# A linear-attention kernel with two MLPs: the opening in another order, y moved between SBUF tiles, the later parts two steps on

## The chip, the cores and the metric

The kernel runs on one core of one Trainium2 chip. The metric is the time of one execution in device microseconds (us); the time before is the median of three runs. The engines are TensorE (PE, with its weight loads PEld), VectorE (DVE), ScalarE (ACT), GpSimd (POOL) and SyncE (SP), which here only issues DMA transfers.

## The reference

```python
def attn(q, k, v, alpha):          # B=4, H=8, S=768, D=48
    for t in range(S):
        state = alpha[:, :, t, :, None] * state + einsum('bhd,bhe->bhde', k[:, :, t], v[:, :, t])
        y[:, :, t] = einsum('bhd,bhde->bhe', q[:, :, t], state)
x = y.transpose(0, 2, 1, 3).reshape(3072, 384)
h = x @ w_in;   x = (h * sigmoid(1.702 * h)) @ w_out        # d_ff = 2048
h = x @ w_in2;  x = (h - tanh(h)) @ w_out2
```

## The kernel before, in words

The 768 tokens of each of the four batches are cut into six **chunks** of 128 tokens, 24 chunks in all. A chunk's attention is done with matmuls. DVE runs two scans over alpha (`a_scan`, L241), and scales k and q with the results (`a_scale`, L247 and L248, "the scale" below). PE makes the scores of the eight heads in two halves (`a_scores`, L277), ACT copies them out of PSUM (L282, L290), POOL masks them (L287). PE then makes the chunk's y and its share of the state (`a_out`, L306, L313, L322, "the sums" below), DVE updates the state (`a_state`, L333 to L336), ACT copies y out (`a_evac`, L341), and y goes by DMA into the DRAM tensor `xt` and from there, transposed, into the tile `xlo` (`a_back`, L359). ACT rounds it into `xhi` (L363), DVE leaves the remainder in `xlo` (`a_x`, L364). `a_guard` (L252, on ACT) squares the scanned alphas for a check at the end.

The two MLPs run behind and beside this in **steps**: one step is one block of 512 tokens (four chunks) with one of the sixteen tiles of 128 hidden columns; there are 6 x 16 steps for each MLP. A step `s` is `gemm1` (nine matmuls, L373: x and the weights are each split into a high and a low part of a shorter format, and three products are made), the activation on ACT (`sig_1`, L387), the split of its result (`g_split`, ACT L390 and DVE L391), and, three steps later, `gemm2` (nine matmuls, L380). `gemm1` of step s writes PSUM bank 3 or 4 in turn, so step s+2 needs the bank that the activation of step s has read.

The weights come as 64-bit numbers, a tile of 768 KB for each of the sixteen, into three `raw` buffers in turn (`w_load`, L154). DVE makes them into 32-bit numbers (`w_bits`, L161 and L162; `w_join`, L174, after which the `raw` buffer is free), ACT rounds the high part (L191), DVE subtracts the low part (L192). These four DVE instructions and the one of ACT are a **conversion**; in the first sixteen steps `conv` makes one in each step.

The code ahead of the steps is the **opening**: chunks 0 to 3, which fill the first block, and the first conversions. `idle(n)` puts n matmuls into it whose result nobody reads. In the first sixteen steps the parts of chunks 4 to 7 are mixed in (`attend`): a scan and the first half of the scores, a scan and the second half, the sums and the scale of the next chunk. `a_done` copies y out and loads the chunk after the next one. The order of these instructions on each engine is the program's own up to step 15 (`in_order`); after that a scheduler sets it.

All transfers go through SP's queue in program order. Each signals one of eight semaphores (DMAHW0 to DMAHW7); a transfer that gets a semaphore whose last transfer may still be under way waits for that one.

Of the kernel before, what the change touches and what calls it, by code (L numbers as in the profile page):

```python
# [7 lines left out]
F32 = mybir.dt.float32  # L8
# [60 lines left out]
def linear_attention_mlps(ctx, tc, xq, xv, fa, fv, cst, w1, w2, out):  # L69
# [106 lines left out]
    def w_any(l, m):  # L176
# [9 lines left out]
        A.copy(whi[m], f)  # L186
        G.tensor_tensor(out=wlo[m], in0=f, in1=whi[m].bitcast(F32), op=ALU.subtract)

    def w_split(l, m):
        f = cfs[l][m % len(cfs[l])]  # L190
        A.copy(whi[m], f)  # L191
        V.tensor_tensor(out=wlo[m], in0=f, in1=whi[m].bitcast(F32), op=ALU.subtract)  # L192

# [73 lines left out]
        V.tensor_scalar(out=flag, in0=bank[0][:1, :1], scalar1=DP + 255.5, scalar2=None, op0=ALU.is_lt)  # L267


    def a_scores(g, x, b):  # L270
        u = (2 * g + x) % 2
        q, k = qq(g), qkk(g)
        o = [bank[b + hh][:, : 2 * CE].rearrange("p (a t) -> p a t", a=2) for hh in range(2)]
        for i in range(2):
            for hh in range(2):
                r = slice(64 * hh, 64 * hh + D)
                P.matmul(out=o[hh][:, i], lhsT=k[r, 2 * x + i], rhs=q[r, 2 * x + i], start=True, stop=True)  # L277
        s4 = sm[u].rearrange("p (b a t) -> p b a t", b=2, a=2)
        kt = kts[u].rearrange("p (b a t) -> p b a t", b=2, a=2)
        for hh in range(2):  # L280
            if g < FULL:
                A.copy(s4[:, hh], o[hh][:, :, :C])  # L282
            else:
                V.tensor_tensor(out=s4[:, hh], in0=o[hh][:, :, :C], in1=mask.unsqueeze(1).to_broadcast([128, 2, C]), op=ALU.mult)
        if g < FULL:
            s3 = sm[u].rearrange("p (a t) -> p a t", a=4)
            G.affine_select(out=s3, in_=s3, pattern=[[0, 4], [1, C]], channel_multiplier=1, base=1 - C,  # L287
                            compare_op=ALU.is_ge, fill=0.0)
        for hh in range(2):
            A.copy(kt[:, hh], o[hh][:, :, C:])  # L290


    def a_out(g, b):
        c = g % NCH
# [40 lines left out]
            else:  # L335
                V.tensor_tensor(out=state, in0=dl, in1=al, op=ALU.mult)  # L336

    def a_evac(g, b):
        ys = ysb[g % 2 if g < FULL else 0]
        for hh in range(2):  # L340
            A.copy(ys[:DP, 2 * C * hh : 2 * C * hh + 2 * C], bank[b + hh][:DP, : 2 * C])  # L341
        y4 = ys.rearrange("p (b a t) -> p b a t", b=2, a=2)
        tk = slice(g * C, g * C + C)
        for n in range(2):
            for hh in range(2):
# [10 lines left out]
    def a_back(g):  # L356
        _, xl, o = a_at(g)
        tk = slice(g * C, g * C + C)
        SP.dma_start(out=xl[:, :, o].bitcast(F32), in_=xt.rearrange("h d t -> (h d) t")[:, tk].rearrange("(k p) t -> p k t", p=128))  # L359

    def a_x(g):
        xh, xl, o = a_at(g)
        A.copy(xh[:, :, o], xl[:, :, o].bitcast(F32))  # L363
        V.tensor_tensor(out=xl[:, :, o], in0=xl[:, :, o].bitcast(F32), in1=xh[:, :, o].bitcast(F32), op=ALU.subtract)  # L364


    def gemm1(i, m, h, n):
        xh, xl = xhi[i % 2], xlo[i % 2]
# [78 lines left out]
    def fetch():  # L447
        while due:
            w_load(*due.pop(0))

    def conv(layer, split=True):
        if split and cv[2] < cv[1]:
            w_split(layer, cv[2] % MT)
            cv[2] += 1
        if cv[1] < cv[0]:
            m = cv[1] % MT
            w_join(layer, m)
            cv[1] += 1
            if m + 3 < MT:
                due.append((layer, m + 3))  # L460
            if layer == 2:
                fetch()
        if cv[0] < min(layer * MT, cv[2] + len(cfs[layer])):
            w_bits(layer, cv[0] % MT)
            cv[0] += 1
# [11 lines left out]
    def a_done(g, b=5):  # L477
        a_evac(g, b)
        if g + 2 < NG:
            a_load(g + 2)  # L480
        if g < FULL:
            a_back(g)

    def attend(g, r, b=5):
        if r == 0:
# [28 lines left out]
    a_load(1, (0, 1))  # L514
    a_load(0, (4,))
    a_load(1, (2, 3, 4))
    a_load(2)
    w_load(1, 0)
    for b in (0, 1, 7):
        V.memset(bank[b], 0.0)  # L520
    V.memset(state, 0.0)
# [2 lines left out]
    for r in range(3):  # L524
        prep(0, r)
    idle(20)
    for g in range(4):
        for r in range(2):
            a_scores(g, r, (5, 3)[r])
        idle(6)  # L530
        if g == 2:
            w_bits(1, 0)
            w_join(1, 0)
            cv[:2] = 1, 1
        if g < 3:
            for r in range(3):
                prep(g + 1, r)
        if g == 3:
            conv(1)
            a_x(0)  # L540
            a_x(1)
            conv(1)
            prep(4, 0)
            prep(4, 1)
        a_guard(g)
        a_out(g, 0)
        idle((8, 4, 10, 36)[g])
# [32 lines left out]
    for s in range(NS + LAG):  # L580
# [19 lines left out]
        if s < NS:  # L600
            if l == 1 and j + 1 < len(L1):
                t1, n1 = L1[j + 1]
                if j:
                    parts, span = n1 // C * 4, 11
                    todo = range(min(parts, -(-m * parts // span)), min(parts, -(-(m + 1) * parts // span)))
                else:
                    todo = ((4 * (m // 3) + m % 3,) if m % 3 < 2 else (4 * (m // 3) + 2, 4 * (m // 3) + 3)) if m < 12 else ()
                for r in todo:
                    attend(t1 // C + r // 4, r % 4)
            if l == 1 and j == 0:  # L610
                sig_1(s, h, n)
                if m % 3 == 2 and m < 12:
                    a_done(m // 3 + 4)
                    a_state(m // 3 + 4)
                if m % 3 == 0 and 0 < m < 13:
                    prep(m // 3 + 4, 3)
                if m % 3 == 1 and m > 3:
                    a_x(m // 3 + 3)
# [138 lines left out]
```

## Time and profile before

| what | us |
|---|---|
| median of 3 runs | 958.71 (957.57 to 959.43) |
| the profiled execution's own time | 958.45 |
| its span in the profile | 956.4 |
| PE busy | 935.7 (98%) |
| DVE busy | 600.8 (63%) |
| ACT busy | 463.5 (48%) |

The shares are means over the whole span. The stretch that the change touches is the first 135 us of the 956, and there the engines stand otherwise to each other than in the mean: tables by stretch and rows in order of time show it. "Idle before" in a row is the pause of that engine ahead of the instruction, with what ended it. PEclk is the share of the full TensorE clock that was granted: 1.00 is 2.4 GHz, 0.50 is 1.2 GHz.

### The profile page before, as it was taken

The numbers are of one execution on the slowest core, as the hardware profiler recorded it, in microseconds if no ns is written. First come the engines' busy times: TensorE is split into PE (matmuls) and PEld (weight loads), VectorE is DVE, ScalarE is ACT, GpSimd is POOL, SyncE is SP. The second block draws the span as 40 slices with busy tenths as digits, with TensorE's granted clock in tenths as the row PEclk, the third lists the DMA queues.
The fourth block names the chain that finished last, engine by engine and source line by source line (L and its number), as shares of the span: only waits on it lengthen the run. The fifth ranks groups of instructions, "written<-read, shape, count | busy, mean of one in ns | idle before, by whom it ended". The sixth has DMA issues, their size and how long they took to land.

```text
span 956.4 us, 13247 instructions
## 1 busy us (share of the span) xinstructions
PE 935.7 (98%) x4972; PEld 726.5 (76%) x4972; DVE 600.8 (63%) x900; ACT 463.5 (48%) x970; POOL 86.6 (9%) x70
## 2 busy tenths in 40 slices
PE   8879999999999999999999999999999999999997
PEld 4457777777777777777788888888888888888885
DVE  6799954442454344733159986766777777766663
ACT  4455534434434444434344555545656656544542
POOL 2111211110110110010100200100101001000000
PEclk9979999999999999999999999999999999999999
DMA  9877423341635545741225400200322420000001
GB/s 231 243 242 233 135 72 106 85 130 41 211 114 186 159 129 177 279 115 50 80 103 168 159 37 1 96 5 0 131 90 78 165 99 1 34 1 1 34 1 38
DMA packets 58042, 101.84 MB, mean 106 GB/s; under 512 B 4992, under 2 KB 37376, under 8 KB 57968
## 3 DMA queue, kind: packets, MB, share of 16 engines
q1 hardware_dynamic: 57968, 100.90, 33.7%
q8 instruction: 41, 0.67, 0.3%
q14 instruction: 33, 0.27, 0.1%
HBM read 86.73 MB, written 14.16 MB: 105 GB/s over the span
## 4 chain that ended last, share of the span: by engine, by line
PE 93%; DVE 2%; DMA 2%; ACT 1%; issue 1%; POOL 0%; SPq 0%; DVEq 0%; ACTq 0%
PE bank L380 43%; PE bank L373 42%; PE bank L277 4%; PE bank L313 2%; PE bank L306 1%; PE bank L322 1%; DMA arena<-xq 1%; DMA cs<-cst 1%; POOL arena L287 0%; DMA xlo<-xt 0%; DVE arena L241 0%; DVE cf L174 0%; DVE cf L162 0%; DVE wlo L192 0%; DVE xlo L364 0%
## 5 line engine op out<-in xcount | busy, mean ns | idle before, releaser
L391 DVE TENSOR_TENSOR glo<-gt,ghi 128x512 fp32r<-128x512 f32 x192 | 139.4, 726 | 170.0 <-ACT ghi L390 166.8
L373 PE MATMUL bank<-xhi,whi 128*128 128x512 f32 x576 | 230.1, 400 | 1.9 <-ACT xhi L363 1.9
L373 PE MATMUL bank<-xlo,whi 128*128 128x512 f32 x576 | 229.1, 398 | 2.4 <-DVE xlo L364 2.4
L380 PE MATMUL bank<-ghi,whi 128*128 128x512 f32 x576 | 230.4, 400 | 0.0
L380 PE MATMUL bank<-ghi,wlo 128*128 128x512 f32 x576 | 229.2, 398 | 0.0
L373 PE MATMUL bank<-xhi,wlo 128*128 128x512 f32 x576 | 228.6, 397 | 0.0
L380 PE MATMUL bank<-glo,whi 128*128 128x512 f32 x576 | 228.2, 397 | 0.0
L390 ACT CAST ghi<-gt 128x512 fp32r<-128x512 f32 x192 | 119.4, 622 | 188.4 <-DVE gt L402 130.2
L373 PEld LDWEIGHTS bank<-xhi,whi 128*128 128x128 f32 x576 | 108.6, 189 | 30.2 <-ACT xhi L363 2.4
L373 PEld LDWEIGHTS bank<-xlo,whi 128*128 128x128 f32 x576 | 108.6, 189 | 29.0 <-DVE xlo L364 2.9
L380 PEld LDWEIGHTS bank<-ghi,whi 128*128 128x128 f32 x576 | 108.6, 189 | 27.6 <-issue 2.7
L373 PEld LDWEIGHTS bank<-xhi,wlo 128*128 128x128 f32 x576 | 108.7, 189 | 26.1 <-issue 0.2
L380 PEld LDWEIGHTS bank<-glo,whi 128*128 128x128 f32 x576 | 108.6, 189 | 26.0 <-issue 0.6
L380 PEld LDWEIGHTS bank<-ghi,wlo 128*128 128x128 f32 x576 | 108.7, 189 | 25.7 <-issue 0.2
L387 ACT ACTIVATE gt<-bank 128x512 f32<-128x512 f32 x96 | 57.5, 599 | 64.9 <-PE bank L373 63.5
L400 DVE SCALAR_TENSOR_TENSOR arena<-arena,bank 128x512 f32<-128x512 f32 x96 | 65.9, 686 | 31.6 <-ACT arena L398 30.6
L241 DVE TENSOR_TENSOR_SCAN arena<-arena,seg 112x516 f32<-112x516 f32 x46 | 61.8, 1343 | 23.4 <-DMA arena<-xq 21.8
L398 ACT ACTIVATE arena<-bank 128x512 f32<-128x512 f32 x96 | 57.6, 600 | 38.7 <-PE bank L373 38.3
L402 DVE SCALAR_TENSOR_TENSOR gt<-arena 128x512 f32<-128x512 f32 x96 | 68.3, 711 | 9.8
L399 ACT ACTIVATE arena<-arena,cs 128x512 f32<-128x512 f32 x96 | 69.7, 726 | 2.9
L401 DVE SCALAR_TENSOR_TENSOR arena<-arena 128x512 f32<-128x512 f32 x96 | 68.2, 710 | 3.0
L439 POOL TENSOR_TENSOR xlo<-arena,xhi 128x512 fp32r<-128x512 f32 x18 | 28.1, 1592 | 355.2 <-ACT xhi L438 355.2
(86 smaller groups left out, 679.7 us busy)
## 6 DMA issues: line engine op xcount, KB each, us to landing
raw<-w SPq DMA_DIRECT2D x64, 768.0 KB, 4.5
arena<-xq SPq DMA_DIRECT2D x46, 224.0 KB, 3.2
arena<-xq SPq DMA_DIRECT2D x22, 451.5 KB, 6.2
xlo<-xt SPq DMA_DIRECT2D x24, 192.0 KB, 4.2
x1t<-xs SPq DMA_DIRECT2D x6, 768.0 KB, 5.1
arena<-x1t SPq DMA_DIRECT2D x6, 768.0 KB, 4.8
out<-xs SPq DMA_DIRECT2D x18, 256.0 KB, 2.3
arena<-xv SPq DMA_DIRECT2D x23, 192.0 KB, 2.7
```

Source lines behind the costliest of these rows:

```text
L241: V.tensor_tensor_scan(out=dec(g, n), data0=src(g, n), data1=seg, initial=0.0, op0=ALU.mult, op1=ALU.max)
L277: P.matmul(out=o[hh][:, i], lhsT=k[r, 2 * x + i], rhs=q[r, 2 * x + i], start=True, stop=True)
L373: P.matmul(out=h, lhsT=w[m][:, ws], rhs=x[:, k, :n], start=c == 0, stop=c == 3 * KT - 1)
L380: P.matmul(out=acc[k][:, :n], lhsT=w[m][:, ws], rhs=x[s % 3][:, :n], start=m == 0 and c == 0, stop=m == MT - 1 and c == 2)
L387: A.activation(out=gf[i][:, :n], in_=h, func=AF.Silu, scale=1.702)
L390: A.copy(ghi[s % 3][:, :n], gf[s % 2][:, :n])
L391: e.tensor_tensor(out=glo[s % 3][:, :n], in0=gf[s % 2][:, :n], in1=ghi[s % 3][:, :n].bitcast(F32), op=ALU.subtract)
L398: A.activation(out=u, in_=h, func=AF.Square, accum_out=usum[:, s - NS1 :][:, :1])
L399: A.activation(out=w, in_=u, func=AF.Square, bias=pbias)
L400: V.scalar_tensor_tensor(out=p, in0=u, scalar=P3, in1=h, op0=ALU.mult, op1=ALU.mult)
L401: V.scalar_tensor_tensor(out=p, in0=u, scalar=-PR, in1=p, op0=ALU.add, op1=ALU.mult)
L402: V.scalar_tensor_tensor(out=gf[i], in0=w, scalar=PD, in1=p, op0=ALU.add, op1=ALU.mult)
```

## The change

1. Scores run one chunk ahead of the sums: chunk g+1 is scanned, scaled and its scores' matmuls are issued ahead of the sums of chunk g. `a_scores` is cut into matmuls (`s_mm`) and copies (`s_copy`).
2. The conversions of the first weight tiles move behind the scale of chunk 3, and they are cut finer (`w_hi`, `w_lo`). Loads: chunk 3 now stands ahead of the first weight tile.
3. y goes from the tile `ysb` straight into `xlo` by ten transfers a chunk (a head has 48 rows, and a head that crosses the tile's 128 rows takes two), where it went by four into `xt` and came back by one. In the opening chunk 3's ten are issued by ACT, all others by SP. This holds for chunks 4 to 23 too.
4. In the first sixteen steps the parts of chunks 4 to 7 stand two steps later (step m takes what step m-2 took), and `conv` stands at the end of a step. The opening now makes three whole conversions and part of a fourth, and chunk 4's scans and scale stand behind them.
5. The opening's idle matmuls go from 102 to 45. A one-element Silu at the start takes the activation table's load there.

```diff
-    def a_evac(g, b):
+    def a_evac(g, b, e=SP):
         ...
-        for n in range(2):
-            for hh in range(2):
-                SP.dma_start(out=xt[2 * n + hh :: 4, :, tk].rearrange("h d t -> d h t"), in_=y4[64 * n : 64 * n + D, hh])
+        _, xl, o = a_at(g)
+        for h in range(H):
+            r = 64 * (h // 2 % 2)
+            at = h * D
+            while at < h * D + D:
+                k, p = divmod(at, 128)
+                n = min(h * D + D - at, 128 - p)
+                e.dma_start(out=xl[p : p + n, k, o].bitcast(F32), in_=y4[r : r + n, h % 2, h // 4])
+                r, at = r + n, at + n
         if g >= FULL:
-            a_back(g)
             a_x(g)
...
-    a_load(0, (0, 1, 2, 3))
+    a_load(0, (0,))
     SP.dma_start(out=cs, in_=cst)
...
+    a_load(3, (0, 2, 3))
+    w_load(1, 0)
     for g in range(4):
-        for r in range(2):
-            a_scores(g, r, (5, 3)[r])
-        idle(6)
+        if g < 3:
+            for r in range(2):
+                prep(g + 1, r)
+            ...
+            prep(g + 1, 2)
+            ...
+            for r in range(2):
+                s_mm(g + 1, r, (5, 3)[r])
         if g == 2:
-            w_bits(1, 0)
+            conv(1)
             w_join(1, 0)
...
+        if g == 3:
+            a_state(2)
+            w_hi(1, 0)
+            for n in range(2):
+                x_hi(n)
+            conv_bits(1)
+            w_join(1, 1)
+            cv[1] = 2
+            w_lo(1, 0)
+            w_hi(1, 1)
+            ...
+        a_out(g, 0)
+        idle((2, 2, 4, 12)[g])
         if g < 3:
-            for r in range(3):
-                prep(g + 1, r)
...
+            for x in range(4):
+                s_copy(g + 1, x % 2, (5, 3)[x % 2], x > 1)
+        a_evac(g, 0, A if g == 3 else SP)
...
-    a_back(3)
-    conv(1)
-    a_x(2)
-    prep(4, 2)
-    a_x(3)
-    fetch()
-    a_load(5)
-    conv(1)
+    w_load(1, 3)
+    a_load(4)
+    ...
+    x_hi(3)
+    a_guard(3)
+    x_lo(3)
+    w_join(1, 2)
+    cv[1] = 3
+    conv_bits(1)
+    w_split(1, 2)
+    cv[2] = 3
+    w_load(1, 4)
+    a_load(5)
+    w_load(1, 5)
+    for r in range(3):
+        prep(4, r)
+        if r == 1:
+            a_state(3)
     prep(4, 3)
...
-                    todo = ((4 * (m // 3) + m % 3,) if m % 3 < 2 else (4 * (m // 3) + 2, 4 * (m // 3) + 3)) if m < 12 else ()
+                    q, r = divmod(m - 2, 3)
+                    todo = () if not 0 <= q < 4 else (4 * q + r,) if r < 2 else (4 * q + 2, 4 * q + 3)
```

Three places show the new order. In the rows `whi_63` is weight tile 0's high part and `wlo_79` its low part, and so on upward; `raw_95` to `raw_97`, `cf_100` to `cf_102` and `xs` are buffers of the conversion; `xhi_103`, `xlo_105` belong to the first block; `bank_126`, `bank_127` are PSUM banks 3 and 4. The scans are listed as SCALAR_TENSOR_TENSOR of 112x516.

SP's queue in the opening, from the second weight tile's load to the third's, before:

```order
L154 DMA raw_96<-w 128x1536 [waits DMAHW7_49]
L346 DMA xt<-wtb 48x2x128 [waits DMAHW0_49,Activation_49]
L346 DMA xt<-wtb 48x2x128 [waits DMAHW1_49,Activation_49]
L346 DMA xt<-wtb 48x2x128 [waits DMAHW2_49]
L346 DMA xt<-wtb 48x2x128 [waits DMAHW3_49]
L359 DMA xlo_105<-xt 128x3x128 [waits DMAHW4_49]
L154 DMA raw_97<-w 128x1536 [waits DMAHW5_49]
```

The same place after, chunk 1's y in both:

```order
L154 DMA raw_96<-w 128x1536 [waits DMAHW5_49]
L366 DMA xlo_105<-wtb 48x128 [waits DMAHW6_49,Activation_49]
L366 DMA xlo_105<-wtb 48x128 [waits DMAHW7_49,Activation_49]
L366 DMA xlo_105<-wtb 32x128 [waits DMAHW0_49]
L366 DMA xlo_105<-wtb 16x128 [waits DMAHW1_49]
L366 DMA xlo_105<-wtb 48x128 [waits DMAHW2_49]
L366 DMA xlo_105<-wtb 48x128 [waits DMAHW3_49]
L366 DMA xlo_105<-wtb 16x128 [waits DMAHW4_49]
L366 DMA xlo_105<-wtb 32x128 [waits DMAHW5_49]
L366 DMA xlo_105<-wtb 48x128 [waits DMAHW6_49]
L366 DMA xlo_105<-wtb 48x128 [waits DMAHW7_49]
L154 DMA raw_97<-w 128x1536 [waits DMAHW0_49]
```

Ten transfers stand between two weight loads where five stood; the eighth of the ten waits for the semaphore of the weight load ahead of them (DMAHW5).

ACT's queue at the end of the opening, from chunk 3's x to the first activation of the MLP, before:

```order
L363 CAST xhi_103<-xlo_105 128x3x128 x2
L191 CAST whi_65<-cf_102 128x768
L252 ACTIVATE arena,guard<-arena 112x1032
L191 CAST whi_66<-xs 128x768
L282 COPY arena<-bank_128 128x256
L282 COPY arena<-bank_129 128x256
L290 COPY arena<-bank_128 128x96
L290 COPY arena<-bank_129 128x96
L387 ACT_TABLE_LOAD
L387 ACTIVATE gt<-bank_126 128x512
```

The same stretch after:

```order
L378 CAST xhi_103<-xlo_105 128x3x128 x2
L259 ACTIVATE arena,guard<-arena 112x1032
L190 CAST whi_65<-cf_102 128x768
L259 ACTIVATE arena,guard<-arena 112x1032
L409 ACTIVATE gt<-bank_126 128x512
L412 CAST ghi_108<-gt 128x512
```

The second guard is that of chunk 4; the copies of chunk 4's first scores, which stood ahead of the first activation, are now two steps behind it, and a conversion's cast less stands there.

DVE's queue over the same time, from chunk 3's x (the L364 of which the second is chunk 3's) to the scale's neighbours, before:

```order
L364 TENSOR_TENSOR xlo_105<-xlo_105,xhi_103 128x3x128
L247 TENSOR_TENSOR arena<-arena 112x512
L248 TENSOR_TENSOR arena<-arena 112x4x128
L364 TENSOR_TENSOR xlo_105<-xlo_105,xhi_103 128x3x128
L192 TENSOR_TENSOR wlo_81<-cf_102,whi_65 128x768
L174 SCALAR_TENSOR_TENSOR xs<-raw_95,xs 128x768
L161 TENSOR_SCALAR xs<-raw_96 128x768
L162 SCALAR_TENSOR_TENSOR xs<-raw_96,xs 128x768
L192 TENSOR_TENSOR wlo_82<-xs,whi_66 128x768
```

After:

```order
L382 TENSOR_TENSOR xlo_105<-xlo_105,xhi_103 128x3x128
L174 SCALAR_TENSOR_TENSOR cf_102<-raw_97,cf_102 128x768
L161 TENSOR_SCALAR xs<-raw_95 128x768
L162 SCALAR_TENSOR_TENSOR xs<-raw_95,xs 128x768
L194 TENSOR_TENSOR wlo_81<-cf_102,whi_65 128x768
L247 MEMSET seg 112x4
L248 SCALAR_TENSOR_TENSOR arena<-arena,seg 112x516
L250 RECIPROCAL seg<-arena 112x4
L248 SCALAR_TENSOR_TENSOR arena<-arena,seg 112x516
L349 TENSOR_TENSOR state<-bank_130,state 112x192
L350 TENSOR_TENSOR state<-state,arena 112x192
L254 TENSOR_TENSOR arena<-arena 112x512
```

Chunk 4's scans and scale, of which the scans stood ahead of chunk 3's x, now stand behind it and behind a conversion.

## Rows read from the trace of the kernel before

**Rows 1.** Stretches: us, PE, PEld, DVE, ACT, POOL busy (instructions), PEclk, DMA share, GB/s.

```profile
0.00:46.60 46.60, 39.83 (x342) 20.82 (x342) 34.35 (x54) 20.72 (x62) 8.85 (x12) 1.00 0.88 233
46.60:53.60 7.00, 4.49 (x11) 2.76 (x11) 6.93 (x11) 2.76 (x5) 0.00 (x0) 0.52 1.04 328
74.10:118.00 43.90, 43.90 (x297) 33.68 (x296) 42.50 (x56) 23.78 (x56) 8.88 (x7) 1.00 0.61 184
118.00:954.00 836.00, 831.59 (x4219) 657.25 (x4217) 496.95 (x754) 403.70 (x821) 65.44 (x48) 1.00 0.28 91
```

**Rows 2.** PE in order of time: start us, us, instruction, [idle before <- what ended it].

```profile
46.68 0.69 PE L373 MATMUL bank<-xhi,whi 128*128 128x512 f32 x1 [1.93 <-ACT xhi L363]
49.80 0.79 PE L373 MATMUL bank<-xlo,whi 128*128 128x512 f32 x1 [2.43 <-DVE xlo L364]
...
68.68 1.54 PE L277 MATMUL bank<-arena 48*128 48x176 f32 x8 [4.63 <-issue]
...
74.15 0.40 PE L373 MATMUL bank<-xhi,whi 128*128 128x512 f32 x1
...
103.59 0.87 PE L277 MATMUL bank<-arena 48*128 48x176 f32 x8
...
118.09 0.40 PE L373 MATMUL bank<-xhi,whi 128*128 128x512 f32 x1
...
122.28 0.39 PE L373 MATMUL bank<-xhi,whi 128*128 128x512 f32 x1
```

**Rows 3.** Issues from 11.4, 33.8, 38.8 us: count, KB each, us to landing.

```profile
raw<-w SPq DMA_DIRECT2D x1, 768.0 KB, 9.6
...
raw<-w SPq DMA_DIRECT2D x1, 768.0 KB, 4.9
...
xt<-wtb SPq DMA_DIRECT2D x4, 48.0 KB, 1.7
```

**Rows 4.** SP's queue in order of time, chunk 5's y.

```profile
83.41 1.77 SPq L346 DMA_DIRECT2D xt<-wtb  x4
```

**Rows 5.** ACT in order of time, end of the opening.

```profile
46.12 0.51 ACT L363 CAST xhi<-xlo 128x384 fp32r<-128x384 f32 x1 [1.71 <-DMA xlo<-xt]
46.53 0.83 ACT L191 CAST whi<-cf 128x768 fp32r<-128x768 f32 x1
49.31 1.07 ACT L252 ACTIVATE arena<-arena 112x1032 f32<-112x1032 f32 x1 [1.95 <-DVE arena L248]
...
55.46 1.28 ACT L387 ACT_TABLE_LOAD   x1
56.76 0.60 ACT L387 ACTIVATE gt<-bank 128x512 f32<-128x512 f32 x1
```

**Rows 6.** DVE in order of time, steps 3 to 7.

```profile
67.29 0.69 DVE L247 TENSOR_TENSOR arena<-arena 112x512 f32<-112x512 f32 x1
...
68.50 0.35 DVE L333 TENSOR_TENSOR state<-bank,state 112x192 f32<-112x192 f32 x1
...
69.16 0.95 DVE L192 TENSOR_TENSOR wlo<-cf,whi 128x768 fp32r<-128x768 f32 x1
...
84.42 0.69 DVE L247 TENSOR_TENSOR arena<-arena 112x512 f32<-112x512 f32 x1
...
85.63 0.95 DVE L192 TENSOR_TENSOR wlo<-xs,whi 128x768 fp32r<-128x768 f32 x1
86.50 0.95 DVE L174 SCALAR_TENSOR_TENSOR cf<-raw,cf 128x768 int32<-128x768 int32 x1
87.36 0.56 DVE L161 TENSOR_SCALAR cf<-raw 128x768 int32<-128x768 int32 x1
...
88.83 0.68 DVE L391 TENSOR_TENSOR glo<-gt,ghi 128x512 fp32r<-128x512 f32 x1
...
90.54 1.23 DVE L241 TENSOR_TENSOR_SCAN arena<-arena,seg 112x516 f32<-112x516 f32 x1 [1.01 <-DMA arena<-xq]
```

**Rows 7.** The page's groups: all scans of that kind, busy us, mean ns.

```profile
L241 DVE TENSOR_TENSOR_SCAN arena<-arena,seg 112x516 f32<-112x516 f32 x46 | 61.8, 1343 | 23.4 <-DMA arena<-xq 21.8
```

More of the change, by code (lines that the diff above doesn't have):

```diff
@@ L277, in a_scores, with s_copy @@
                 P.matmul(out=o[hh][:, i], lhsT=k[r, 2 * x + i], rhs=q[r, 2 * x + i], start=True, stop=True)
+    def s_copy(g, x, b, turned):
+        u = (2 * g + x) % 2
+        o = [bank[b + hh][:, : 2 * CE].rearrange("p (a t) -> p a t", a=2) for hh in range(2)]
         s4 = sm[u].rearrange("p (b a t) -> p b a t", b=2, a=2)
         kt = kts[u].rearrange("p (b a t) -> p b a t", b=2, a=2)
+        if turned:
+            for hh in range(2):
+                A.copy(kt[:, hh], o[hh][:, :, C:])
+            return
         for hh in range(2):
@@ L449, in fetch, with conv_bits @@
             w_load(*due.pop(0))
+    def conv_bits(layer):
+        w_bits(layer, cv[0] % MT)
+        cv[0] += 1
     def conv(layer, split=True):
@@ L517, in linear_attention_mlps @@
     a_load(2)
-    w_load(1, 0)
+    A.activation(out=fine[:1, :1], in_=seg[:1, 1:2], func=AF.Silu)
     for b in (0, 1, 7):
@@ L526, in linear_attention_mlps @@
     idle(20)
-    for g in range(4):
-        for r in range(2):
-            a_scores(g, r, (5, 3)[r])
-        idle(6)
+    a_guard(0)
+    for r in range(2):
+        s_mm(0, r, (5, 3)[r])
+    for x in range(4):
+        s_copy(0, x % 2, (5, 3)[x % 2], x > 1)
+    idle(5)
+    a_load(3, (0, 2, 3))
+    w_load(1, 0)
+    for g in range(4):
+        if g < 3:
+            for r in range(2):
+                prep(g + 1, r)
+            if g == 1:
+                a_state(0)
+                a_guard(1)
+            prep(g + 1, 2)
+            if g == 2:
+                a_state(1)
+                a_guard(2)
+            for r in range(2):
+                s_mm(g + 1, r, (5, 3)[r])
@@ L550, in linear_attention_mlps @@
+        a_out(g, 0)
+        idle((2, 2, 4, 12)[g])
+        if g < 3:
+            for x in range(4):
+                s_copy(g + 1, x % 2, (5, 3)[x % 2], x > 1)
+        a_evac(g, 0, A if g == 3 else SP)
         if g == 0:
-            a_load(3)
+            a_load(3, (4,))
             w_load(1, 1)
-        if g:
-            a_back(g - 1)
         if g == 1:
             w_load(1, 2)
-            a_load(4)
-        if g == 2:
-            w_load(1, 3)
-    a_back(3)
-    conv(1)
-    a_x(2)
@@ L563, in linear_attention_mlps @@
-    prep(4, 2)
-    a_x(3)
-    fetch()
-    a_load(5)
-    conv(1)
+    w_load(1, 3)
+    a_load(4)
+    for n in range(2):
+        x_lo(n)
+    x_hi(2)
+    x_lo(2)
+    w_lo(1, 1)
+    cv[2] = 2
+    x_hi(3)
[3 more added lines that the diff above has]
+    cv[1] = 3
+    conv_bits(1)
+    w_split(1, 2)
+    cv[2] = 3
+    w_load(1, 4)
+    a_load(5)
+    w_load(1, 5)
[3 more added lines that the diff above has]
+            a_state(3)
     prep(4, 3)
@@ L611, in linear_attention_mlps @@
                 sig_1(s, h, n)
[L612 to L618, printed above, removed]
+                q, r = divmod(m - 2, 3)
+                if r == 2 and 0 <= q < 4:
+                    a_done(q + 4)
+                    a_state(q + 4)
+                if r == 0 and 0 < q < 5:
+                    prep(q + 4, 3)
+                if r == 1 and q > 0:
+                    a_x(q + 3)
+                conv(1)
+                fetch()
             if 2 <= j < 4 and m % 2:
```

52 lines of the change are left out of this document (22 added, 30 removed).

## The prediction

> **What bounds the kernel now.** I read the table by stretch first, then PE's rows in order of time, then the queues that PE waits for. From 74.1 us on PE pauses for nothing that counts: 43.90 us busy of 43.90, then 831.59 of 836 [rows 1]. So the opening cannot change the time through anything but one thing: how much earlier PE gets the same work done in its first steps. Ahead of that stand the pauses. The first matmul of step 0 starts at 46.68, waits 2.43 us for DVE's x, and starts again at 49.80; step 3 ends and PE stands still for 4.63 us up to the scores at 68.68 [rows 2]. After the first pair of pauses PEclk is 0.52, that is half clock, for seven us [rows 1]. The engine behind the second pause is DVE: 42.50 us busy of 43.90 in the steps that follow [rows 1], and the scale of chunk 5, which those scores need, starts on it at 67.29 [rows 6]. In these steps, then, **PE and DVE are nearly level**, and this decides how much of an earlier start can be kept.
>
> **The landmark.** I measure by the first scores of chunk 7. Before they start at 103.59, in step 9 [rows 2]; after they stand in step 11. The chunk parts ahead of them are the same, so the changed kernel has by then made two more steps of gemm1 and gemm2. A step without parts is 122.28 - 118.09 = 4.19 us [rows 2]. If PE runs without pauses behind the landmark in both, and S is its start in the changed kernel, the gain is 8.4 - (S - 103.6).
>
> **When step 0 starts (T).** SP's queue leads here. All transfers share eight semaphores, so the eighth of a chunk's ten y transfers waits for the weight load ahead of it, and the next weight load stands behind them all. The loads of chunks 0 to 2 are the same as before. Before, the first weight tile lands at 11.4 + 9.6 = 21.0 [rows 3]; now chunk 3's 900 KB stand ahead, at the 233 GB/s of this stretch [rows 1] 3.9 us, so 24.9. An issue on SP costs 1.77 / 4 = 0.44 us [rows 4]: three y and one load of v later, at 26.7, the second tile is issued and lands 4.9 us later [rows 3] at 31.6. Three y more, and the third tile is issued at 32.9 and lands at 37.8. The last y of chunk 1 lands 1.7 us [rows 3] behind its issue, 34.6. ACT then makes that x (0.51), a cast of weights (0.83) [rows 5] and two copies of y (0.5, my estimate from the shorter of these), and issues chunk 3's ten at 36.5. The third of them waits for the third weight tile, 37.8; eight at 0.44 end at 41.3, and they land at 43.0. Beside them a weight tile and chunk 4's loads move: I add 0.5, an estimate. One cast, 0.51, gives T = 44.0 against 46.68. The bounds are 42.0 (the weights land 1 us sooner each) and 46.7 (nothing won). By the Trainium skill's page on DMA: Bandwidth & Descriptors, section "Issuing engines are not separate DMA queues", issuing from ACT saves only the time of issuing; no row here shows ACT issuing, so the addition of 0.5 stays an estimate.
>
> **From T to gemm1 of step 2.** This step needs bank 3, so the first activation; on ACT it stands behind chunk 4's guard, which waits for chunk 4's scale. In DVE's new order there lie behind T: x's low part (0.5, estimated as half a weight tile's 0.87), join 86.50 to 87.36, bits 87.36 to 88.83, weights' low part 85.63 to 86.50 [rows 6], two scans at 1.34 [rows 7], the state 68.50 to 69.16, the scale 67.29 to 68.50 [rows 6]: 0.5 + 0.9 + 1.5 + 0.9 + 2.7 + 0.7 + 1.2 = 8.3. Then guard 1.07 and activation 0.60 [rows 5]: T + 10. PE has made steps 0 and 1 at half clock by then (2 x 4.2) and waits some two us, **a new pause in the place of those before**. The table load of 1.28 [rows 5] that stood here is at the start now, beside ACT's wait for the first data; it gives nothing by itself, since DVE's scale ends last.
>
> **From there to the landmark, by PE alone.** gemm1 of step 2 at half clock 4.2, gemm1 of step 3 and gemm2 of step 0 4.2, the four parts that before were over at 74.15 (three of scores at 0.87 [rows 2] and one of sums, about 2): 4.6; the work from 74.15 to 103.59, 29.4; two steps, 8.4. Sum: T + 10.2 + 50.8 = T + 61.0.
>
> **The same by DVE.** Before, DVE needs 84.42 - 67.29 = 17.1 us from one scale to the next [rows 6]: three conversions, three low parts of the activation, two scans, a state, an x and a scale. After: scale 4 at T + 8.3. Up to scale 5 there are four joins and bits and four low parts, but no state and no x: 17.1 + 2.4 + 0.6 - 1.2 = 18.9. Up to scale 6: 17.1. Up to scale 7, no state (chunk 5 ends its batch): 16.4. Sum T + 60.7. To it come two waits of a scan for its data, one chunk each; the nearest row shows 1.01 [rows 6], so 2.0, and two short ones for ACT's casts behind the guard, 0.7 (an estimate from a cast of 0.83). T + 63.4. **DVE is last**, by 2.4 us: PE pauses ahead of the scores of chunks 6 and 7. S = 44.0 + 63.5 = 107.5, and the gain is 8.4 - 3.9 = 4.5. After a pause of 1.93 and 2.43 the clock was halved [rows 1, 2]; I count one such stretch, nine matmuls, 2.1 us. **Gain 2.4 us.** Bounds of the price of that stretch: nothing, and 4.2 if it comes twice.
>
> **Edits at no price.** Fifty-seven fewer idle matmuls: nobody waits for them; the longer pause ahead of T is why I count steps 0 to 2 at half clock. Chunks 8 to 23: five transfers become ten on SP, and ACT waits for one landing where it waited for two; PE's 831.59 of 836 [rows 1] covers them, as a block's x is wanted a whole block later. If that cover failed in places, it would be of the size of one landing, 1.7, either way; it widens the range by 1. The first scores wait for constants that now come sooner and for q that comes later: 0.5 at most, ahead of a queue that waits for weights anyway.
>
> **Rivals.** *First: the loads come late (slower).* `a_done` puts a chunk's ten y transfers ahead of the load of the chunk after next: 4.4 us of issues where 1.77 stood [rows 4], 2.7 later, so a scan that waited 1.01 [rows 6] could wait 3.7, at two chunks. S = 107.5 + 5.4 = 112.9, the gain is -0.9, and two pauses of four us each are followed by half clock, 4.2: 5.1 slower, 963.8. It decides from 4.4 us of such waits in all, where the gain is gone. For it: the scan at 90.54 already waits with four [rows 6]. Against it: DVE itself comes late in the new order, so the data have longer. The Trainium skill speaks for it (DMA: Bandwidth & Descriptors, section "Rules for kernel authors"): many small transfers should be one large one, since under 64 KB one pays mostly overhead; the row of four 48 KB transfers that land 1.7 us after issue [rows 3] agrees that their bytes (0.2 us of 233 GB/s) are the small part, and this is the one reason why I give it more than a tenth.
>
> *Second: the opening is no sooner.* If chunk 3's y lands late, T = 46.7, S = 110.2, the gain 1.8 - 2.1: 959.0, no change. For it: the chain to T has two weight loads in a row, and each was up to 9.6 [rows 3]. It is also the case in which the change does not do what it says.
>
> *Third: DVE is not late.* Without the waits of 2.7, PE sets S at T + 61.0 = 105.0, and no pause halves the clock: 7.0 gained, 951.7. For it: the scan data may come in time, since chunk 5's load is issued in the opening. Against it: PE and DVE differ by only 0.3 in the sum, so any of DVE's longer instructions undoes it.
>
> **How the numbers follow.** The profiled execution took 958.45 with a span of 956.4; I forecast its span at 954.0. The difference of 2.05 stays, and the execution lies within 0.3 of the median 958.71. The predicted time is 958.7 - 2.4 = 956.3. Chances: forecast (gains of 0.7 to 5) 0.45, the loads late 0.18, no sooner 0.20, DVE not late 0.17. Range: 951.5 takes in most of the third rival; 961.0 takes in the second with the wider bounds and the near half of the first; two in ten stay outside. A change within 0.2%, 1.9 us, cannot be told from none. Faster by more: two thirds of the forecast (0.29), the third rival (0.17) and 0.02 of the second: 0.48. Slower by more: the first (0.18), 0.02 each of the forecast and the second: 0.22. Within: the rest, 0.30.
>
> **What would show it.** The start of step 0 near 44 in PE's rows, and SP's y transfers pausing in front of weight landings, show T. A pause of PE ahead of gemm1 of step 2 that ACT's activation ends, shows the new wait. DVE's scales 17 us apart, and PE pausing ahead of scores by one to two us, show that DVE sets the landmark; its start at 107.5 is the test. Scan waits over 2 us for `xq` would show the first rival. I am wrong altogether if PE pauses behind step 16, or if the landmark is early and the end is not.

## The result and the profile after

The changed kernel takes 969.47 us (967.08 to 970.79, four runs) beside 958.67 for the kernel before; the ratio is 1.0111 with an interval of 1.0088 to 1.0134. It is **slower by 10.8 us**, where 2.4 us of gain were forecast. The profiled execution took 970.06, its span is 968.3; before these were 958.45 and 956.4, so in the trace the loss is 11.9.

The stretches that answer to [rows 1]; columns as there, from the trace after:

```profile
0.00:46.60 46.60, 28.94 (x285) 17.80 (x285) 28.62 (x45) 19.00 (x58) 7.49 (x12) 0.85 0.66 164
46.60:74.10 27.50, 15.54 (x63) 11.42 (x64) 19.36 (x29) 11.01 (x24) 1.32 (x2) 0.75 0.75 231
74.10:118.00 43.90, 39.82 (x267) 29.96 (x266) 36.44 (x52) 21.32 (x49) 4.35 (x4) 0.96 0.59 186
118.00:954.00 836.00, 832.70 (x4270) 660.18 (x4269) 516.28 (x771) 409.10 (x836) 70.67 (x52) 1.00 0.28 89
```

Behind 118 us PE is as full as before (832.70 of 836, before 831.59). So nearly all of the loss stands ahead of it, and DVE, 42.50 us busy of 43.90 before, has 7.5 us of idle time there now. PE's rows that answer to [rows 2]: the start of step 0, gemm1 of step 2, and the scores of chunk 7, the landmark, with the pause behind it.

```profile
55.30 0.80 PE L395 MATMUL bank<-xhi,whi 128*128 128x512 f32 x1 [17.65 <-ACT xhi L378]
...
65.39 0.50 PE L395 MATMUL bank<-xhi,whi 128*128 128x512 f32 x1 [3.26 <-ACT gt L409]
...
102.86 0.87 PE L283 MATMUL bank<-arena 48*128 48x176 f32 x8 [1.72 <-issue]
...
123.02 0.87 PE L283 MATMUL bank<-arena 48*128 48x176 f32 x8 [1.94 <-issue]
...
133.18 0.50 PE L395 MATMUL bank<-xhi,wlo 128*128 128x512 f32 x1 [1.36 <-DVE wlo L194]
```

Step 0 starts at 55.30 and not at 46.68: 8.6 us late. The landmark is at 123.02, so by the prediction's own accounting the gain is 8.4 - (123.0 - 103.6) = -11.0. **8.6 of the 11.0 are step 0's late start**, and 2.4 come between it and the landmark. The pause of 1.36 at 133.18 stands behind the landmark, outside this accounting. The waits of DVE ahead of it, which answer to [rows 6], and the group of [rows 7]:

```profile
90.94 1.23 DVE L248 TENSOR_TENSOR_SCAN arena<-arena,seg 112x516 f32<-112x516 f32 x1 [3.10 <-DMA arena<-xq]
...
110.91 1.23 DVE L248 TENSOR_TENSOR_SCAN arena<-arena,seg 112x516 f32<-112x516 f32 x1 [4.02 <-DMA arena<-xq]
```

```profile
L248 DVE TENSOR_TENSOR_SCAN arena<-arena,seg 112x516 f32<-112x516 f32 x46 | 64.0, 1392 | 35.4 <-DMA arena<-xq 33.8
```

Why step 0 is late stands in SP's queue, in order of time (in the rows of L366 `arena` and `wtb` are the two buffers of y):

```profile
16.00 0.35 SPq L154 DMA_DIRECT2D raw<-w  x1
22.25 7.64 SPq L366 DMA_DIRECT2D xlo<-arena  x10
29.98 0.53 SPq L243 DMA_DIRECT2D arena<-xv  x1
30.56 0.43 SPq L154 DMA_DIRECT2D raw<-w  x1
31.09 7.66 SPq L366 DMA_DIRECT2D xlo<-wtb  x10
38.79 0.58 SPq L154 DMA_DIRECT2D raw<-w  x1
39.47 7.63 SPq L366 DMA_DIRECT2D xlo<-arena  x10
47.20 0.53 SPq L154 DMA_DIRECT2D raw<-w  x1
48.05 0.34 SPq L237 DMA_DIRECT2D arena<-xq  x1
```

and on ACT, at the same time:

```profile
40.04 0.51 ACT L378 CAST xhi<-xlo 128x384 fp32r<-128x384 f32 x1 [6.52 <-DMA xlo<-wtb]
...
41.59 7.47 ACTq L366 DMA_DIRECT2D xlo<-wtb  x10
49.23 0.51 ACT L378 CAST xhi<-xlo 128x384 fp32r<-128x384 f32 x1 [7.40 <-DMA xlo<-wtb]
54.74 0.51 ACT L378 CAST xhi<-xlo 128x384 fp32r<-128x384 f32 x1 [5.00 <-DMA xlo<-wtb]
```

The same row of ACT from its third issue on, and the first two weight tiles, issued at 16.00 and 30.56, with their us to landing:

```profile
43.70 5.36 ACTq L366 DMA_DIRECT2D xlo<-wtb  x8
...
raw<-w SPq DMA_DIRECT2D x1, 768.0 KB, 10.1
...
raw<-w SPq DMA_DIRECT2D x1, 768.0 KB, 6.4
```

The view of line 366 gives each issue (ns, least, median and most) and its way to landing:

```profile
L366 SPq DMA_DIRECT2D xlo<-arena x200: 503/587/1907, 22.2 to 479.5; - x100
...
DMA to landing us min/median/max: 1.7/1.8/6.4
```

A chunk's ten transfers hold their queue for 7.6 us: ten issues of 0.587 are 5.9, the rest is waiting between them. The fourth cast of x, which step 0 needs, waits until 54.74 for chunk 3's y. Its last transfers were issued by 49.1, behind a weight load (SP, 47.20) and beside chunk 4's loads (48.05 on): they are those with 6.4 us to landing.

### The profile page after: what moved, and what is told of

The parts are those of the page before. It is cut to its first block, busy times and chain, and to the rows that moved or that the text cites. A ratio compares the mean times of both kernels' runs of the same rounds, so it can differ in the third digit from the quotient of the medians.

```text
span 968.3 us, 13440 instructions
## 1 busy us (share of the span) xinstructions
PE 924.5 (95%) x4915; PEld 724.6 (75%) x4915; DVE 603.7 (62%) x900; ACT 462.1 (48%) x970; POOL 83.8 (9%) x70
## 4 chain that ended last, share of the span: by engine, by line
PE 87%; DMA 4%; DVE 4%; SPq 2%; ACT 1%; issue 1%; DVEq 0%; ACTq 0%
PE bank L402 40%; PE bank L395 39%; PE bank L283 3%; DMA arena<-xq 3%; PE bank L329 2%; SPq L366 2%; DVE arena L248 1%; PE bank L322 1%; PE bank L338 1%; DVE wlo L194 1%; DMA xlo<-arena 1%; DMA raw<-w 1%; DVE cf L174 0%; ACT ghi L412 0%; DVE glo L413 0%
## 5 line engine op out<-in xcount | busy, mean ns | idle before, releaser
L248 DVE TENSOR_TENSOR_SCAN arena<-arena,seg 112x516 f32<-112x516 f32 x46 | 64.0, 1392 | 35.4 <-DMA arena<-xq 33.8
```

Source lines behind the costliest of these rows:

```text
L248: V.tensor_tensor_scan(out=dec(g, n), data0=src(g, n), data1=seg, initial=0.0, op0=ALU.mult, op1=ALU.max)
```

## The experiments

Theory A: the number of y transfers is what costs, by their issues and by what stands behind them. Theory B: the order of the opening and the parts two steps later cost. Theory C: only the last two transfers, queued behind loads, cost.

**e1, y through DRAM in the changed kernel.** All else is as changed.

```diff
...
-                e.dma_start(out=xl[p : p + n, k, o].bitcast(F32), in_=y4[r : r + n, h % 2, h // 4])
...
+        for n in range(2):
+            for hh in range(2):
+                e.dma_start(out=xt[2 * n + hh :: 4, :, tk].rearrange("h d t -> d h t"), in_=y4[64 * n : 64 * n + D, hh])
...
+            a_back(g)
...
```

> The changed kernel with y through DRAM again: four transfers to xt and one back, as before; all else is as changed. Theory A, the ten transfers: in the changed kernel SP takes 7.6 us for a chunk's ten (0.63 us each, and lane waits), and ACT's x conversions and chunk 3's copy stand behind their landing. Five at 0.44 us are 2.2, so step 0 starts at 43 to 46 in the place of 55.3, and the two scan waits for xq of 3.1 and 4.0 us fall to the 1 us of before: 11 to 13 us off the 969.5, 956 to 959. Theory B, the order of the opening: scores one chunk ahead put the first y copy on ACT at 21.8 (14.5 before), and parts two steps later hold DVE; the way of y matters little, and the trip back is one landing more: step 0 at 52 or later, 966 to 970.

956.1 us, ratio 0.9985 (0.9972 to 0.9999): all of the loss is gone, and 1.4 us more. PE's two pauses and the view of the four transfers' line:

```profile
45.00 0.80 PE L396 MATMUL bank<-xhi,whi 128*128 128x512 f32 x1 [8.67 <-ACT xhi L379]
57.95 0.80 PE L396 MATMUL bank<-xhi,whi 128*128 128x512 f32 x1 [6.58 <-ACT gt L410]
```

```profile
L362 SPq DMA_DIRECT2D xt<-arena x80: 327/428/1092, 21.5 to 459.4; - x80
```

Step 0 starts 10.3 us sooner than in the changed kernel, no scan of chunks 4 to 7 waits for xq, and the landmark is at 109.93: a gain of 2.1 by the accounting. Theory A holds, B falls.

**e2, the direct transfers alone in the kernel before.** The mirror of e1: the same lines the other way; all ten are issued by SP, chunk 3's too.

> The kernel before with the ten direct transfers alone, no other edit. Theory A: SP issues ten at 0.63 for four at 0.44 and one back, three or more us a chunk in the opening; step 0 starts 5 to 8 us later than 46.7, the loads of later chunks stand behind the ten, scans wait 3 to 4 us: 965 to 969. Theory B: one landing less for each chunk, so no slower than before: 956 to 960.

971.1 us, ratio 1.0126 (1.0104 to 1.0149), above the range that A gave and above the whole change. Step 0 starts at 52.61, and the same scans wait:

```profile
81.82 1.23 DVE L241 TENSOR_TENSOR_SCAN arena<-arena,seg 112x516 f32<-112x516 f32 x1 [3.97 <-DMA arena<-xq]
...
101.93 1.23 DVE L241 TENSOR_TENSOR_SCAN arena<-arena,seg 112x516 f32<-112x516 f32 x1 [3.97 <-DMA arena<-xq]
```

So this one part costs 12 to 13 us in either kernel (958 x 0.0126 here; 969.5 - 956.1 there), and the other parts together are worth about 1.4 us (0.1 to 2.7 by the interval of e1), where 2.4 were forecast for the whole.

**e5, ten transfers to DRAM.** e1 with y written to DRAM in the changed kernel's ten pieces, and read back by one transfer. It separates the number from the path.

```diff
-        for n in range(2):
-            for hh in range(2):
-                e.dma_start(out=xt[2 * n + hh :: 4, :, tk]...
+                e.dma_start(out=to[p : p + n, k], in_=y4[r : r + n, h % 2, h // 4])
```

> The kernel of e1 (y through DRAM) with y written out in the ten pieces of the changed kernel in the place of four; the way back is one transfer, as in e1. It separates the number of transfers from their path. If the number is what costs, SP takes 10 x 0.6 + 0.4 us a chunk in the place of 2.2, step 0 starts past 50 and scans wait 3 us or more for xq: 968 to 978, as slow as the changed kernel or slower by the landing more. If the path from SBUF to SBUF is what costs, it stays by e1: 955 to 960.

969.65 us, ratio 1.0125 (1.0103 to 1.0147). Step 0 starts at 53.77, scans wait 2.14 and 2.87, a little less than expected. With ten pieces the way through DRAM costs what the direct way costs, with four it does not. The path is not what costs; **the number is**, and with it the size of the pieces, which no run here changes alone.

**e4, the loads behind the last y.** The changed kernel with the fourth weight load and chunk 4's loads on ACT's queue, behind chunk 3's ten.

```diff
-    w_load(1, 3)
-    a_load(4)
+    w_load(1, 3, A)
+    a_load(4, e=A)
```

> The changed kernel with the fourth weight load and chunk 4's loads issued on ACT's queue behind chunk 3's ten y transfers, so that none of the ten stands behind them. Theory C, the last two transfers: in the changed kernel they are issued at 47.9 and 48.4 and land at 54.2 and 54.6, behind 768 KB of weights and chunk 4; without these they land 1.8 us after issue, so step 0 starts at 51 to 52: 965 to 966. Theory A: most of the time is in the issues ahead (step 0 still at 51 or later), and chunk 4's data come 2 us later to DVE, which gives back half of it: 967 to 969.

967.75 us, ratio 1.0103 (1.0086 to 1.0120): the time that A gave, but not clear of the changed kernel's 1.0111 (1.0088 to 1.0134). Step 0 starts at 51.54, 3.8 sooner. Most of this isn't the edit's doing, and the edit didn't clear the way:

```profile
38.99 7.51 ACTq L366 DMA_DIRECT2D xlo<-wtb  x10
...
44.65 0.53 SPq L154 DMA_DIRECT2D raw<-w  x1
```

ACT's ten begin at 38.99, where they began at 41.59, ahead of the first line that e4 changes. With the very opening of the changed kernel they begin at 37.64 in e3 and at 40.39 in e10 below. So the time from ACT's first issue to step 0 is what can be compared: 13.7 us in the changed kernel, 13.6 in e3, 13.5 in e10, and 12.6 here. **The edit is worth 1 us of step 0, not 3.8.** On SP the fifth weight tile moved up into the gap, to 44.65, and so a weight tile still stands ahead of the last two y transfers. They land 4.1 and 3.7 us after issue (6.4 and 6.2 in the changed kernel), not 1.8. What the last two would gain with no load ahead of them, theory C, is not shown by any run. The total gains less than 2, since DVE waits as before (3.21 and 3.92 us for xq).

**e9 and e10, the ten in the steps alone and in the opening alone.** e9: chunks 0 to 3 through DRAM, the others direct; e10, with `g < 4`: the other way round.

```diff
+        if g >= 4:
...
+                    e.dma_start(out=xl[p : p + n, k, o].bitcast(F32), in_=y4[r : r + n, h % 2, h // 4])
...
+        else:
...
+                    e.dma_start(out=xt[2 * n + hh :: 4, :, tk].rearrange("h d t -> d h t"), in_=y4[64 * n : 64 * n + D, hh])
```

> Between e1 and the changed kernel: chunks 0 to 3 by way of DRAM (as e1), chunks 4 to 23 by ten direct transfers (as changed). It gives the share of the ten in the steps. If a chunk's loads that stand behind the ten set DVE back, step 0 starts at 45 as in e1, the scans of chunks 6 and 7 wait 3 to 4 us each for xq, and the scores of chunk 7 come 4 to 6 us later than in e1: 960 to 963. If the whole cost lies in the opening: within 1.5 us of e1, 955 to 957.5.

> The other half: chunks 0 to 3 by ten direct transfers (as changed), chunks 4 to 23 by way of DRAM (as e1). If the two halves of the cost add up, step 0 starts at 51 to 55, no scan waits more than 1.5 us for xq, and what is lost against e1 is the rest of some 13 us beside e9's: 962 to 966. If the wait of the scans in the changed kernel was only a consequence of the late step 0, e9 is free and this one costs it all: 967 to 970.

e9: 962.54 us, ratio 1.0046 (1.0030 to 1.0063). Step 0 starts at 45.57 as in e1, and the scans wait:

```profile
84.43 1.23 DVE L248 TENSOR_TENSOR_SCAN arena<-arena,seg 112x516 f32<-112x516 f32 x1 [3.22 <-DMA arena<-xq]
...
104.19 1.23 DVE L248 TENSOR_TENSOR_SCAN arena<-arena,seg 112x516 f32<-112x516 f32 x1 [3.81 <-DMA arena<-xq]
```

e10: 961.49 us, ratio 1.0034 (1.0023 to 1.0044), a little under its range; the profiled execution, the longest of its ten runs, starts step 0 at 53.89, and a scan waits 0.64. By the ratios the halves lie 0.61% and 0.49% above e1, together 10.5 us, against 1.26%, 12 us, for both in one kernel: they nearly add up. **About half of the loss is the opening, half the steps.** One theory is out with that: the scans' waits are no mere consequence of a late step 0, since e9 has them with step 0 on time.

**e3, the load ahead of the ten.** The changed kernel with one swap in `a_done`.

```diff
-        a_evac(g, b)
         if g + 2 < NG:
             a_load(g + 2)
+        a_evac(g, b)
```

> The changed kernel with one swap: in the steps, the load of the chunk after next is issued ahead of the ten y transfers, not behind them; the opening is the same. Theory A says that in the steps the ten cost by what stands behind them on SP: the scan waits of 3.1 and 4.0 us fall under 1 us, step 0 stays at 55.3, scores of chunk 7 come at 117 to 119 in the place of 123.0, 963 to 966. Theory B (DVE is late by the parts two steps later, and waits for xq only fill its slack): the waits go, the scores of chunk 7 stay within 1.5 us of 123, 968 to 970.

965.8 us, ratio 1.0079 (1.0062 to 1.0095), in A's range, but not by A's working alone. The scan waits are gone, and the landmark stands at 112.72 with step 0 at 51.23: 61.5 us between them in the place of 67.7. Step 0 was 4.1 sooner without an edit to the opening, as said at e4. By the accounting the landmark stands for a loss of 0.7, the span for 7.7, so what was won between the two is given back behind it. One piece is a pause of PE. In DVE's order both scans of chunk 9 stand here ahead of the low part that PE waits for, where in e1 they stand behind it, and DVE works up to it without a pause; the scan below takes 2.17 in the place of 1.23. Another piece is seen at e6.

```profile
129.94 2.17 DVE L248 TENSOR_TENSOR_SCAN arena<-arena,seg 112x516 f32<-112x516 f32 x1
...
133.55 0.95 DVE L194 TENSOR_TENSOR wlo<-cf,whi 128x768 fp32r<-128x768 f32 x1
```

```profile
134.55 0.50 PE L395 MATMUL bank<-xhi,wlo 128*128 128x512 f32 x1 [2.50 <-DVE wlo L194]
```

**e6, the parts back at their old steps.** e1 with the parts of chunks 4 to 7 two steps sooner; the line stands twice.

```diff
-                    q, r = divmod(m - 2, 3)
+                    q, r = divmod(m, 3)
```

> The kernel of e1 with the parts of chunks 4 to 7 back at the steps at which they stood before (two steps sooner in the order); conversions and the opening are as in e1. By the accounting of the prediction (DVE sets the scores of chunk 7, and the two steps ahead of them are what is won) PE waits in front of step 1 for chunk 4's scale, and again at chunk 5 to 7, with two steps fewer to fill it: 3 to 8 us slower than e1, 959 to 964. If the parts two steps later won nothing, it stays within 1.5 us of e1: 955 to 957.5.

964.43 us, ratio 1.0076 (1.0055 to 1.0096): slower than e1 by a little more than expected, and not for the reason given. The landmark is at 101.91, in step 9 again, a gain of 1.7 by the accounting, beside 2.1 for e1: **up to the landmark the two steps later are worth next to nothing by themselves**; DVE sets the scores in both. The loss lies behind it. The kernel before has its landmark in the same step, 9, so the two can be compared from there to the end, e6 ahead of the kernel before:

```profile
101.91:962.70 860.79, 851.75 (x4326) 671.64 (x4326) 515.50 (x779) 413.95 (x843) 72.55 (x52) 1.00 0.29 92
...
103.59:956.44 852.85, 846.00 (x4327) 668.53 (x4326) 511.22 (x770) 411.74 (x841) 71.17 (x52) 1.00 0.28 91
```

Of the 7.9 us more, 5.8 are PE's busy time for the same work, and 2.2 are two waits for weights (1.62 and 0.56). The parts of chunks 8 on stand in another order. The order is written out by hand only for the opening and steps 0 to 15; behind it the scheduler that builds the program sets it, and in e6 it breaks groups of eight matmuls into fours. The groups of PE from 120 to 480 us, e6 ahead of e1:

```profile
L283 PE MATMUL bank<-arena 48*128 48x176 f32 x256 | 33.7, 336 | 0.0
```

```profile
L283 PE MATMUL bank<-arena 48*128 48x176 f32 x256 | 30.0, 335 | 0.0
```

The same 256 score matmuls take 3.7 us more. e3 has 32.3 for them. So the ends of e3 and e6 hold a few us that come from the scheduler's order and not from the waits that were tried; the landmark does not hold them. That the edits set off this order is likely, and not shown. In the kernel before (30.6) and the changed one (31.5 for 272) they cost what they cost in e1, to within a microsecond.

**e7 and e12, chunk 4's work sooner.** e1 had left a pause of 6.58 us in front of step 2. In e7, chunk 4's load is issued ahead of the last transfer back, its scans, state and scale stand on DVE between the conversions, and its guard on ACT stands behind the first activation. e12 is the same kernel again.

```diff
+    a_load(4)
     a_back(3)
     w_load(1, 3)
-    a_load(4)
...
+    prep(4, 0)
+    prep(4, 1)
+    a_state(3)
     x_hi(3)
     a_guard(3)
     x_lo(3)
+    prep(4, 2)
...
                 sig_1(s, h, n)
+                if m == 0:
+                    prep(4, 3)
```

> The kernel of e1 with chunk 4's load ahead of the last transfer back and of the fourth weight load, chunk 4's two scans, state and scale on DVE between the conversions (where DVE waits 2.9 and 2.5 us in e1), and chunk 4's guard on ACT behind the first activation. If the 6.6 us that PE waits in front of step 2 and DVE's late start are what is left to win, that pause goes, DVE's scale of chunk 4 ends at 49 to 53 (56.2 in e1) and that of chunk 7 as much sooner: 2 to 4 us below e1, 952 to 954. If the load's 900 KB hold up the last y by as much as is won: within 1 us of e1.

> The kernel of e7 once more, with more rounds and beside e11 on one chip: 951.6 was the median of four runs. If that stands, 950 to 953, 5 to 7 us below the kernel before.

951.64 us, ratio 0.9934 (0.9912 to 0.9956), a little under the range, and again 953.41, ratio 0.9957 (0.9941 to 0.9974), a little above it. Step 0 starts 3.4 us later than in e1 and the landmark 3.1 sooner (106.80). The pause in front of step 2 is gone; PE waits a little for DVE's scales:

```profile
48.41 0.79 PE L396 MATMUL bank<-xhi,whi 128*128 128x512 f32 x1 [11.51 <-ACT xhi L379]
72.66 0.87 PE L283 MATMUL bank<-arena 48*128 48x176 f32 x8 [0.76 <-issue]
89.63 0.87 PE L283 MATMUL bank<-arena 48*128 48x176 f32 x8 [0.56 <-issue]
```

An earlier step 0 is not the aim by itself, then; the three edits together bring the scale of chunk 4 forward and win. Which of them wins how much is not shown. The kernel is faster than the one before and the changed one.

**e11, idle matmuls back.** e7 with `idle(50)` in the place of `idle(12)` ahead of step 0.

> The kernel of e7 with fifty idle matmuls in the place of twelve ahead of step 0, so that PE works until about 46 us. It tests the prediction's sentence that the idle matmuls taken out cost nothing but half clock in steps 0 to 2. In e7 the granted clock is half from 39.7 to 53.3, and some eleven matmuls of steps 0 and 1 start 0.43 us apart in the place of 0.23. If PE sets the time there: up to 2 us below e7. If DVE's scale of chunk 5, for which e7's scores at 72.66 wait, ends last: within 1 us of e7.

951.2 us, ratio 0.9938 (0.9918 to 0.9957), beside 953.41 for e12; the two intervals overlap. From step 0 to the landmark it is 58.0 us (46.28 to 104.27), in e12 57.9 (48.85 to 106.78). But the edit didn't give step 0 the full clock: the idle matmuls end at 43.4 and not at 46, and the granted clock, still 1.00 when step 0 starts, is half for 3.4 us from 47.80 on. In e12 it is half up to 54.3. e11 ahead of e12 (the column behind POOL is PEclk):

```profile
47.80:51.20 3.40, 3.40 (x10) 2.68 (x9) 3.37 (x6) 2.16 (x3) 0.00 (x0) 0.51 1.02 358
...
48.85:54.30 5.45, 5.45 (x13) 4.08 (x13) 5.42 (x8) 2.88 (x5) 0.00 (x0) 0.50 1.01 350
```

So two us less at half clock win nothing up to the landmark, as if DVE ended last; what the full clock would give isn't shown. What differs in the two totals is ahead of the idle matmuls, where the two programs are the same. There the granted clock falls at different times, e11 ahead of e12:

```profile
20.40:27.10 6.70, 5.48 (x82) 4.23 (x82) 6.52 (x12) 4.12 (x13) 2.08 (x2) 0.99 0.93 292
...
20.40:27.10 6.70, 6.14 (x62) 5.05 (x64) 4.31 (x7) 1.49 (x4) 1.27 (x2) 0.50 0.92 298
```

Whether the idle matmuls are worth anything is left open.

**e8, scales on POOL.** e7 with the scales of chunks 5 to 7 on POOL.

```diff
-        e = V if g < FULL else G
+        e = V if g < 5 else G
```

> The kernel of e7 with the scales of chunks 5 to 7 on POOL (two of about 1.3 us each, by POOL's rows of chunks 8 on) in the place of DVE (0.69 each). If DVE sets the scores of chunks 5 to 7, it is free 1.4 us sooner in each chunk, POOL's scale is 1.2 us longer once: 1 to 3 us below e7. If PE sets them, no change; if the two engines get in each other's way, DVE's scans and conversions grow beyond 1.23 and 0.95 us and it is slower than e7.

956.36 us, ratio 0.9996 (0.9982 to 1.0010): slower than e7, by the third of the cases expected, the two engines in each other's way. A chunk's scale is two instructions, so six went to POOL. Beside each of the six one of DVE's instructions takes 1.93 to 1.95 us that elsewhere takes 0.94; the first pair:

```profile
61.41 1.89 POOL L254 TENSOR_TENSOR arena<-arena 112x512 f32<-112x512 f32 x1
...
62.17 1.94 DVE L174 SCALAR_TENSOR_TENSOR cf<-raw,cf 128x768 int32<-128x768 int32 x1
```

So DVE gives away 0.69 us of work with each of them and loses 1.0 of time. POOL takes 1.40 to 2.02 us for one, more than the 1.3 of its later rows, and PE now waits in another place, for DVE's low parts of the weights: 5.8 us in six waits.

```profile
PE bank L396 <- DVE wlo L194: 5.8, 6, 1.4
```

## Why the prediction was wrong

**What bounds the kernel: right up to the landmark, not behind it.** PE and DVE are level there, and the landmark's accounting gives the result in one subtraction: -11.0 against 10.8 us lost by the medians, 11.9 in the trace. It also gives e1 (2.1, measured 1.4 to 1.7) and e7 (5.2, measured 4 to 6.3). It doesn't give e2 (-10.5, the span 14.1 longer), e3 (-0.7, 7.7 longer) and e6 (+1.7, 6.3 longer). The prediction put what stands behind the landmark as the same in both kernels; in these three, 3.6 to 8.0 us are lost there.

**The step that failed: the start of step 0.** I put T at 44.0 and its bounds at 42.0 and 46.7; it was 55.3. ACT's third issue did wait for the third weight tile, as the sum had it. Three stretches of the chain were too short.
- *To ACT's first issue, 41.6 in the place of 36.5: 5.1 us.* Of these, 2.7 are weights that landed late: the first tile at 26.1 where I had 24.9, the second after 6.4 us where I had 4.9. The rest is mostly issuing. The row [rows 4] is of four transfers of 48 KB to DRAM; I used its 0.44 for pieces of 24 KB and less into SBUF, which take 0.587 each (median of the view above). And when the first tile landed, six of chunk 0's ten were still to be issued, where I had three: 4.4 us up to the second weight load and not 1.8. This stretch is not the same each time: in e3 and e10, with the same opening, ACT's first issue is at 37.64 and 40.39.
- *From ACT's first issue to the end of its last, 7.5 in the place of 4.8: 2.7 us.* The third piece stood 2.1 us behind the first, waiting for its weight tile, where the sum had 1.3; the eight from it on took 5.36 and not 3.5.
- *From there to the cast: landing in 1.7 us, with 0.5 for company.* The last two took up to 6.4, behind a weight tile and beside chunk 4's loads; the cast that waits for them started at 54.7 where I had 43.5. That is another 3.4. In e4, with chunk 4's loads behind them and a weight tile still ahead, they took 4.1 and 3.7. The Trainium skill has the rule (DMA: Bandwidth & Descriptors, section "Issuing engines are not separate DMA queues"): transfers that ACT and SP issue run on the same DMA engines. The prediction cited it and then allowed 0.5 us for it; the trace agrees with the page: 6.4 us for 24 KB behind what SP had issued.

The second and third stretch are the firm part: from ACT's first issue to step 0 it took 13.5 to 13.7 us in three traces, where the sum had 7.5.

The bound "nothing won", 46.7, was the worse mistake: it had no price for the case that ten transfers hold the queue longer than the trip through DRAM that they replace. e5 shows that this goes with their number and not with their path. The Trainium skill's rule that small transfers should be made into one (DMA: Bandwidth & Descriptors, section "Rules for kernel authors") spoke against this change, and the trace agrees: 7.6 us for some 190 KB in ten pieces, 1.8 for the same in four [rows 4].

**From T to step 2: right.** T + 10.0 was forecast, T + 10.1 came, with a new pause of 3.26 that ACT's first activation ends. In e1, where step 0 is sooner, the same wait is 6.58, and e7 shows that it can be taken away.

**From T to the landmark: the first rival in the place of the forecast.** T + 63.5 was forecast, T + 68.9 the rival's, T + 67.7 came. Its waits were to be 3.7 us at two chunks; they were 3.10 and 4.02. Alone, in e9, they cost 0.46% against the kernel before, 4.4 us; the rival's price was 5.1. I gave it 0.18 and held against it that DVE comes late itself: it does, but y comes as late, and the load stands behind y. The prediction took the two failures as cases that exclude each other. They have one cause, the ten issues, and came together, which no case of the sum had.

**The half clock: one stretch forecast, two came,** the eleven matmuls from 55.3 and another stretch at 104.7 to 108.1 (PEclk 0.50), of 2.2 and 1.6 us.

```profile
39.90:60.30 20.40, 5.00 (x11) 3.80 (x12) 9.30 (x14) 4.70 (x9) 0.00 (x0) 0.50 0.77 226
60.30:104.70 44.40, 37.30 (x241) 27.71 (x240) 40.26 (x59) 22.23 (x53) 3.65 (x5) 1.00 0.57 184
104.70:108.10 3.40, 3.40 (x10) 2.62 (x9) 2.16 (x4) 2.87 (x6) 0.77 (x1) 0.50 0.27 52
```

If DVE ends last, what they cost at the end is less than that; e11, with two us less of the first, wins nothing between step 0 and the landmark.

**Chunks 8 to 23: right.** The scans wait 33.8 us in all, 21.8 before [rows 7], and PE's 832.70 of 836 shows that nobody pays for it there.

**The rest of the change** without the ten ends at 956.1 in e1, next to the 956.3 that was forecast for the whole. That is no credit to the forecast, which was of the ten transfers too.

## What to carry over

Count the transfers, not the bytes and not the trips: a piece costs its queue's issue, and everything that is queued behind. Take the price of an issue from a row of the same size and destination, and let a bound for a new queue order go beyond "nothing won". When two late things have one cause, price them as one case.

## What the runs showed of the hardware that was not expected

- A smaller transfer did not issue faster: 0.587 us for one of at most 24 KB into SBUF (median), 0.428 for one of 48 KB to DRAM.
- SP and ACT issued side by side without slowing each other: SP's ten took 7.63 us while ACT issued its own (7.47), and 7.64 alone. What stands ahead of a transfer shows in its landing, up to 6.4 us in the place of 1.8, behind a weight tile on the other queue.
- A scale on POOL and an instruction of DVE beside it slowed each other: 1.94 us in the place of 0.94 on DVE, 1.40 to 2.02 in the place of 1.3 on POOL (e8).
- In the opening the granted clock falls at different times in runs of the same instructions (0.99 and 0.50 in one stretch of e11 and e12). In three traces of one opening step 0 starts at 55.30, 51.23 and 53.89 (changed kernel, e3, e10), so a single trace shows its start to some 4 us; why it moves is not shown.
